# Second MLP product of a token mixer in eight pairs of token blocks instead of two whole blocks and seven pairs

## The chip, the cores and the metric

The kernel runs on one core of one Trainium2 chip. The metric is the device time of one execution in microseconds; the profile is that of one such execution, and its times count from the first instruction of the span.

## What is computed

The reference modulates and normalizes a sequence x of S = 2048 tokens by D = 640 channels, adds a gated state-space block (A), normalizes again and adds a gated MLP over the token axis (B). The change is in block B:

```python
h = _layernorm(x, axis=-1)                                  # (B, S, D)
u = jnp.einsum("bsd,sf->bdf", h, w1) + b1                  # (B, D, F)
u = _gelu(u)
y = jnp.einsum("bdf,fs->bds", u, w2) + b2                  # (B, D, S)
...
x = x + gb * _B_ref(h, B_w1, B_b1, B_w2, B_b2)
```

with F = 1728. All data is float32.

## The kernel before

A float32 product is made of three matmuls on rounded operands: each operand is split into a rounded part (`hi`, written as F32R by ScalarE) and a rest (`lo`, the difference, by VectorE), and hi x hi, hi x lo and lo x hi are added up in PSUM. Every matmul here has a stationary block of 128x128 and 320 moving columns, that is half of the 640 channels.

**First product.** U, F by D, is made in 14 blocks of F. The normalized tokens stand in SBUF as 16 pairs of tiles `H[j]` (hi and lo) of 640 columns each; H[0] to H[2], H[9] to H[11] lie in a tile named `r_z`, H[3] to H[5] in `r_v`, H[6] to H[8] in `h_a`, H[12] to H[15] in `h_x`. The loop over `FS` makes blocks 4 to 12, one after another (96 matmuls each: 16 j, 3 steps, 2 halves; in the loop's round for block 6 the blocks 6 and 13 are made together). The weights of the next block are loaded into the tile `X` and split meanwhile (`load_w`, `split_w`). `u_evac` takes a block's sums from PSUM through the GELU and stores U[f] as hi and lo, for each half of the channels.

**Second product.** The output is made of 16 token blocks s of 128 tokens. Before the change the first NW = 2 of them are whole blocks: 14 blocks of F, 3 steps, 2 halves, 84 matmuls each (line 1121). The other 14 are made in NP = 7 pairs. A pair, times two halves of F (blocks 0 to 6 and 7 to 13) and two halves of the channels, is a 2 by 2 block product, and is done with seven half-size products instead of eight. Their stationary sides are A11, A12, A22 (blocks of w2) and sums of blocks S1 to S4 (`sums`); their moving sides are parts of U and, for S1, S2, S3 and A22, sums of parts of U, the sets `TU[i]`, i = 0 to 6. One such product is 7 sets by 3 steps, 21 matmuls (line 1057), so a pair has 147.

A set i is made from U[i] and U[7 + i] by `t_sums`: two sums of the upper part, one of the lower, three differences. It has four tiles of 320 columns, held as two pairs: the first serves S1 and S3, the second S2 and A22. There is no room for the sets while H is in use. So sets 6, 0, 1, 2, 3 (`SAVED`) are made during blocks 7 to 11 and written to a DRAM tensor `ts` (`t_save`), whole. Sets 0 to 3 are loaded back into tiles of H (`t_back`) when the last block (f = 12) has read these, and split there during the last block and the first whole token block (`t_split`); sets 4 and 5 are made and split at once (`t_make`). Set 6 is loaded behind the whole blocks (lines 1127 to 1129).

The order on each engine is the order of the code; nothing reorders it. SyncE issues the loads and stores one after another, and each waits, in this queue, for the tile that it writes to be free. For product n, `prep` splits the stationary side into one of three slots (ScalarE, then VectorE), two products ahead. `outcome` takes the product from PSUM, and `finish` (VectorE) adds the bias, multiplies by the gate, adds x (loaded back by `x_load` from DRAM tensor `xs`) and stores a quarter of a pair. PSUM has four slots of two banks, used in turn.

Of the kernel before, what the change touches and what calls it, by code (L numbers as in the profile page):

```python
# [50 lines left out]
def mixer_kernel(ctx: ExitStack, tc: tile.TileContext, q, k, v, shift_k, ssm_k, ssm_D, w1, b1, w2, b2, c,  # L51
# [16 lines left out]
    ts = drp.tile([5 * 128, 1280], F32, name="ts")  # L68
# [315 lines left out]
    NF, NW = 14, 2  # L384
    FS = (4, 5, 6, 7, 8, 9, 10, 11, 12)
    WB = {i: n % 2 for n, i in enumerate(FS + tuple(range(NF, NF + NW)))}
# [3 lines left out]
    f14 = lambda t: t[:, 0:1792].rearrange("p (f m) -> p f m", f=14)  # L390

    def load_w2(t, s, f0, n):

        for h in range(n // 7 or 1):
            o = 7 * h
            sync.dma_start(t[:, o:o + 6, :], dram(w2, fo(f0 + o) * S + 128 * s, [[S, 128], [128 * S, 6], [1, 128]]))
            sync.dma_start(t[:, o + 6, :], dram(w2, fo(f0 + o + 6) * S + 128 * s, [[S, 128], [1, 128]]))

    def load_w(i, t=X):
        if i is None:  # L400
            return
        if i < NF:
            t = j16(t)
            for b in range(2):
                sync.dma_start(t[64 * b:64 * b + 64],
                               dram(w1, 16 * b * F + fo(i), [[32 * F, 64], [F, 16], [1, 128]]))
            raw[i] = (t, [slice(0, 8), slice(8, 16)])
        else:
            t = f14(t)
            load_w2(t, i - NF, 0, 14)  # L410
            raw[i] = (t, [slice(0, 7), slice(7, 14)])
# [14 lines left out]
    def split_w(i, t2=None, eng=dve):  # L426
        if i is None:
            return
        if t2 is None:
            t2 = T_wb[WB[i]]  # L430
        view = j16 if i < NF else f14
        hi, lo = view(t2[:, 0:2048]), view(t2[:, 2048:4096])
# [247 lines left out]
    acc = []  # L680
# [160 lines left out]
    right = thirds(mem("xb", 5120, "u_x"), 14)  # L841
# [33 lines left out]

    def t_sums(i):

        t, w_, u, (hi, lo) = m_p[:, 0:640], m_p[:, 768:2048], U[i], full[7 + i]
        TT(dve, w_[:, 0:320], u[0], u[2], ALU.add)
        TT(dve, w_[:, 320:640], u[1], u[3], ALU.add)  # L880
        TT(dve, w_[:, 640:1280], hi, lo, ALU.add)
        TT(dve, two_(t), span2(w_, 320, 640), span2(w_, 0, 320), ALU.subtract)
        TT(dve, w_[:, 960:1280], w_[:, 960:1280], t[:, 0:320], ALU.subtract)
        TT(dve, w_[:, 640:960], w_[:, 640:960], w_[:, 960:1280], ALU.subtract)
        return two_(t), two_(w_[:, 640:1280])
# [7 lines left out]
    def t_back(i):  # L893

        n = SAVED.index(i)
        for k in range(2):
            sync.dma_start(span2(H[JS[i][k]][0], 320, 640), ts[128 * n:128 * n + 128, 640 * k:640 * k + 640]
                           .rearrange("p (h m) -> p h m", h=2))

    def t_split(i, whole=None):  # L900

        for k in range(2):
            hi, lo = (span2(H[JS[i][k]][0], o, 640) for o in (0, 320))
            act.activation(hi.bitcast(F32R), whole[k] if whole else lo, AF.Copy)
        for k in range(2):
            hi, lo = (span2(H[JS[i][k]][0], o, 640) for o in (0, 320))
            TT(dve, lo.bitcast(F32R), whole[k] if whole else lo, hi, ALU.subtract)

    def t_make(i):
        t_split(i, t_sums(i))  # L910
# [8 lines left out]
    after = dict(zip(FS, FS[1:] + tuple(range(NF, NF + NW))))  # L919
    after.update({i: i + 1 for i in range(NF, NF + NW - 1)})  # L920
# [45 lines left out]
    NP = (16 - NW) // 2  # L966
# [3 lines left out]
    def load_pair(p, n0=0, n1=4):  # L970

        if p < NP:
            for n in range(n0, n1):
                w_ = ("A11", "A21", "A22", "A12")[n]
                A[p, w_] = place[(4 * p + n) % 8]
                load_w2(A[p, w_], NW + 2 * p + int(w_[1] == "2"), 7 * int(w_[2] == "2"), 7)

    for f_ in FS:
# [5 lines left out]
        load_w(13 if f_ == 4 else nxt(n_))  # L984
        if f_ == 6:
            m_p = ends(sets)
            continue
# [6 lines left out]
        if f_ == FS[-1]:  # L994
            m_v = mem("v", 4520, "m_v")
            place = [q7(t, o + 896 * i) for t, n, o in ((m_v, 5, 0), (X, 2, 0), (m_p, 1, 1152)) for i in range(n)]
# [10 lines left out]
    m_w, slots = [], []  # L1007
    S1 = q7(m_p, 0)
    W, bank = {}, {}
    Q = lambda n, i: U[7 * (n // 2) + i]  # L1010
    moving = {"A11": lambda i: Q(0, i)[0::2], "A12": lambda i: Q(2, i)[0::2], "S4": lambda i: Q(2, i)[1::2],
              "S1": lambda i: TU[i][0], "S2": lambda i: TU[i][1], "S3": lambda i: TU[i][2], "A22": lambda i: TU[i][3]}
    ORDER = ("A11", "A12", "S1", "S2", "S3", "S4", "A22")

    def x_load(s, h, t):
        sync.dma_start(t, xs[128 * s:128 * s + 128, 320 * h:320 * h + 320])

    def x_pair(p):
        if p < NP:
            for n in range(4):  # L1020
                x_load(NW + 2 * p + n // 2, n % 2, xq[4 * (p % 2) + n])

    def sums(n):

        p, w_ = n // 7, ORDER[n % 7]
        if p >= NP:
            return
        a = lambda k: A[p, k]
        if w_ == "S1":
            A[p, w_] = S1  # L1030
            TT(dve, S1, a("A21"), a("A22"), ALU.add)
        elif w_ == "S2":
            TT(dve, a("A21"), a("A11"), a("A21"), ALU.subtract)
            TT(dve, a("A11"), S1, a("A11"), ALU.subtract)
            A[p, "S3"], A[p, "S2"] = a("A21"), a("A11")
        elif w_ == "S4":
            TT(dve, a("A12"), a("A12"), a("S2"), ALU.subtract)
            A[p, "S4"] = a("A12")

    def prep(n):  # L1040

        p, w_ = n // 7, ORDER[n % 7]
        if p < NP:
            W[n] = slots[n % 3]
            act.activation(W[n][0].bitcast(F32R), A[p, w_], AF.Copy)  # L1045
            TT(dve, W[n][1].bitcast(F32R), A[p, w_], W[n][0], ALU.subtract)

    def product(n):
        w_ = ORDER[n % 7]
        if n > 4 or n % 2 == 0:  # L1050
            bank["t"] = psum()
        bank[n] = bank["t"][:, 0:320] if n > 3 or n % 2 == 0 else bank["t"][:, 512:832]
        wh, wl = W.pop(n)
        for i in range(7):
            rh, rl = moving[w_](i)
            for k, (w, r) in enumerate(((wh, rh), (wh, rl), (wl, rh))):
                pe.matmul(bank[n], w[:, i].bitcast(F32R), r.bitcast(F32R), start=i == 0 and k == 0,  # L1057
                          stop=i == 6 and k == 2)
# [12 lines left out]
    def outcome(n):  # L1071

        p, w_ = n // 7, ORDER[n % 7]
        t, s, x = bank.pop(n), NW + 2 * p, xq[4 * (p % 2):4 * (p % 2) + 4]
# [8 lines left out]
        elif w_ == "S3":  # L1083
            TT(dve, u3, t, u2, ALU.add)
            TT(dve, u2, u2, p5, ALU.add)
            finish(s + 1, 1, u3, o4, x[3], p5)
# [3 lines left out]
        elif w_ == "S4":  # L1090
            finish(s, 1, t, o2, x[1], u2)
        elif p == NP - 1:
            finish(s + 1, 0, t, o3, u3)
        else:
            finish(s + 1, 0, t, o3, x[2], u3)

    acc = []
    for s in range(NW):
        i = NF + s
        acc.append(psum().rearrange("p (h m) -> p h m", h=2))  # L1100
        split_w(nxt(i))
        load_w(nxt(nxt(i)))
        if s == 0:
            t_make(5)
            t_split(1)
        if s == NW - 1:
            load_pair(1, 0, 3)
            m_w.append(mem(f"w{WB[NF + NW - 2]}", 4096, "m_w0"))
            slots += [(q7(m_w[0], 1792 * i), q7(m_w[0], 1792 * i + 896)) for i in range(2)]
            t_split(2)  # L1110
            t_split(3)
            prep(0)
            prep(1)
            sums(2)
            sums(3)
        wh, wl = blk[i]
        for f_ in range(NF):
            u = U[f_]
            for k, (w, r) in enumerate(((wh, 0), (wh, 2), (wl, 0))):
                for h in range(2):  # L1120
                    pe.matmul(acc[s][:, h, 0:320], w[:, f_].bitcast(F32R), u[r + h].bitcast(F32R),  # L1121
                              start=f_ == 0 and k == 0, stop=f_ == NF - 1 and k == 2)
    m_w.append(mem(f"w{WB[NF + NW - 1]}", 4096, "m_w1"))
    t_ = thirds(m_w[1], 7, 1792) + thirds(m_w[0], 1, 3584)
# [70 lines left out]
```

## Time and profile before

| | us |
|---|---|
| three runs before, median | 698.0 |
| lowest, highest | 696.08, 701.78 |
| profiled execution, its own time | 701.14 |
| its span, first to last instruction | 699.4 |
| last block of the first product (f = 12) ends | 518.0 |
| two whole token blocks (L1121) | 518.0 to 542.7 |
| seven pairs (L1057) | 542.7 to 695.4 |

The mean granted clock of TensorE was 0.974. A row of the timeline has the start, the length, the engine, the line of the code, the operation, the tiles written and read, the shapes and the count, and in brackets how long the engine sat idle before it and what ended that. PE is TensorE, PEld its weight loads, DVE VectorE, ACT ScalarE, POOL GpSimd, SPq the DMA issues of SyncE; L60 is the line of a helper that records every two-operand sum. A row of the windows has the busy time of PE, PEld, DVE, ACT and POOL, each with its count, then the granted clock of TensorE, the share of the DMA engines' time that was busy, and the GB/s that they moved.

### The profile page before, as it was taken

The numbers are of one execution on the slowest core, as the hardware profiler recorded it, in microseconds if no ns is written. First come the engines' busy times: TensorE is split into PE (matmuls) and PEld (weight loads), VectorE is DVE, ScalarE is ACT, GpSimd is POOL, SyncE is SP. The second block draws the span as 40 slices with busy tenths as digits, with TensorE's granted clock in tenths as the row PEclk, the third lists the DMA queues.
The fourth block names the chain that finished last, engine by engine and source line by source line (L and its number), as shares of the span: only waits on it lengthen the run. The fifth ranks groups of instructions, "written<-read, shape, count | busy, mean of one in ns | idle before, by whom it ended". The sixth has DMA issues, their size and how long they took to land.

```text
span 699.4 us, 20705 instructions
## 1 busy us (share of the span) xinstructions
PE 642.1 (92%) x9078; PEld 621.7 (89%) x9078; DVE 499.2 (71%) x844; ACT 308.1 (44%) x463; POOL 155.3 (22%) x137
## 2 busy tenths in 40 slices
PE   0699978899999999987899999999999999999997
PEld 0699678889999999777899999999999999999997
DVE  6778569849779837888895420563477698888886
ACT  0664574435645645555776421521333333333331
POOL 5297049614715626300000000000000000000000
PEclk9999899889999999989899999999999999999999
DMA  9978988527242523352022641466284734455511
GB/s 180 206 217 242 340 164 167 118 47 156 52 79 69 186 60 93 116 121 62 21 40 54 129 92 30 98 133 161 91 254 134 221 115 129 141 172 172 160 49 39
DMA packets 170848, 89.36 MB, mean 128 GB/s; under 512 B 89571, under 2 KB 160518, under 8 KB 170758
## 3 DMA queue, kind: packets, MB, share of 16 engines
q1 hardware_dynamic: 166210, 86.73, 49.2%
q10 hardware_dynamic: 4548, 1.31, 1.1%
q8 instruction: 71, 1.16, 0.7%
q14 instruction: 19, 0.16, 0.1%
HBM read 74.25 MB, written 13.76 MB: 126 GB/s over the span
## 4 chain that ended last, share of the span: by engine, by line
PE 66%; DVE 14%; POOL 8%; ACT 4%; issue 3%; SPq 2%; DMA 2%; ACTq 0%; DVEq 0%; POOLq 0%
PE pst L1057 21%; PE pst L446 17%; PE pst L230 7%; POOL y L60 6%; PE pst L275 5%; PE pst L246 5%; PE pst L1121 4%; PE pst L945 3%; DVE tap L60 3%; PE pst L294 2%; DVE kt L60 2%; POOL t L60 1%; SPq L164 1%; DMA in<-in_A_k_dram 1%; PE tap L354 1%
## 5 line engine op out<-in xcount | busy, mean ns | idle before, releaser
L246 PEld LDWEIGHTS pst<-z,w 128*64 128x64 f32 x2560 | 94.8, 141 | 8.6 <-ACT z L232 7.3
L246 PE MATMUL pst<-z,w 128*64 128x64 f32 x2560 | 95.8, 240 | 7.1 <-ACT z L232 6.1
L60 POOL TENSOR_TENSOR y<-p 128x256 f32<-128x256 f32 x72 | 91.7, 1327 | 23.2 <-DVE p L60 22.9
L60 DVE TENSOR_TENSOR p<-pst,kt 128x512 f32<-128x512 f32 x80 | 52.8, 691 | 23.6 <-ACT kt L250 14.3
L230 PE MATMUL pst<-v,x 128*64 128x128 f32 x640 | 46.7, 308 | 23.6 <-DVE x L60 23.6
L230 PEld LDWEIGHTS pst<-v,x 128*64 128x64 f32 x640 | 44.7, 221 | 24.1 <-POOL t L471 23.6
L232 ACT ACTIVATE z<-pst 128x1024 f32<-128x1024 f32 x40 | 46.0, 1149 | 40.2 <-PE pst L230 21.8
L1057 PE MATMUL pst<-r_z,m_w 128*128 128x320 f32 x259 | 48.5, 309 | 1.5 <-DVE m_w L60 1.5
L275 PEld LDWEIGHTS pst<-v,y 32*128 32x128 f32 x1280 | 41.9, 203 | 7.3 <-POOL y L60 4.4
L275 PE MATMUL pst<-v,y 32*128 32x64 f32 x1280 | 43.9, 290 | 4.1 <-DVE y L60 3.2
L1045 ACT ACTIVATE m_w<-m_v 128x896 fp32r<-128x896 f32 x30 | 27.8, 948 | 43.1 <-DVE m_v L60 27.6
L250 ACT ACTIVATE kt<-pst 128x512 f32<-128x512 f32 x40 | 25.0, 625 | 46.5 <-PE pst L246 24.2
L1057 PEld LDWEIGHTS pst<-r_z,m_w 128*128 128x128 f32 x259 | 40.6, 188 | 1.7 <-DVE m_w L60 1.7
L60 DVE TENSOR_TENSOR m_w<-m_v,m_w 128x896 fp32r<-128x896 f32 x30 | 32.5, 1087 | 11.2 <-ACT m_w L1045 10.8
L230 PE MATMUL pst<-v,p 128*64 128x128 f32 x640 | 37.3, 274 | 2.2 <-ACT p L176 1.6
L230 PEld LDWEIGHTS pst<-v,p 128*64 128x64 f32 x640 | 35.0, 137 | 3.2 <-ACT p L176 1.7
L851 ACT ACTIVATE pst<-pst,sm 128x640 f32<-128x640 f32 x14 | 10.7, 767 | 59.0 <-PE pst L446 59.0
L60 DVE TENSOR_TENSOR tap<-tap,kt 128x512 f32<-128x512 f32 x51 | 35.6, 698 | 1.3
L60 DVE TENSOR_TENSOR kt<-in,tap 128x512 f32<-128x512 f32 x51 | 35.0, 687 | 1.5
L1057 PE MATMUL pst<-h_x,m_w 128*128 128x320 f32 x168 | 33.7, 309 | 0.0
L283 ACT ACTIVATE z<-pst 128x512 f32<-128x512 f32 x38 | 21.4, 664 | 27.1 <-PE pst L275 27.1
L1045 ACT ACTIVATE m_w<-m_p 128x896 fp32r<-128x896 f32 x13 | 12.4, 954 | 44.2 <-DVE m_p L60 27.7
(309 smaller groups left out, 1401.2 us busy)
## 6 DMA issues: line engine op xcount, KB each, us to landing
x<-in_B_w_dram SPq DMA_DIRECT2D x20, 512.0 KB
m_v<-in_B_w_dram SPq DMA_DIRECT2D x19, 384.0 KB
aux<-in_A_ssm_k_dram SPq DMA_DIRECT2D x10, 512.0 KB
m_x<-xs SPq DMA_DIRECT2D x32, 160.0 KB
out_dram<-m_x SPq DMA_DIRECT2D x32, 160.0 KB
in<-in_A_k_dram SPq DMA_DIRECT2D x36, 128.0 KB
in<-in_A_v_dram SPq DMA_DIRECT2D x36, 128.0 KB
x<-in_B_w_dram SPq DMA_DIRECT2D x10, 384.0 KB
```

The lines of the kernel that those rows point to most:

```text
L60: TT = lambda eng, o, a, b, op: eng.tensor_tensor(o, a, b, op=op)
L230: pe.matmul(ps[64 * ri:64 * ri + 64, o:o + 128], lhs, F1[:, 128 * ri:128 * ri + 128], start=True, stop=True)
L232: evac = lambda: act.activation(Z[:, side, t].rearrange("p a k e -> p e a k"), ps.rearrange("p (e a k) -> p e a k", a=8, e=2), AF.Copy)
L246: pe.matmul(ps[64 * h:64 * h + 64, o:o + 64], W2[k1 // 32][:, 2 * (k1 % 32) + ri], rhs, start=True, stop=True)
L250: act.activation(kt.rearrange("p (m i) -> p m i", i=32), pv[:, :, 1], AF.Copy)
L275: pe.matmul(pp[qd // 2][:, o:o + 64], Y[p, ri, i:i + 2].rearrange("p i k -> p (i k)"), V2[p, 64 * ri:64 * ri + 64], start=ri == 0, stop=ri ...
L283: act.activation(o, i, AF.Copy)
L446: pe.matmul(ps[0:m, h, 0:320], w_.bitcast(F32R), r_[:, 320 * h:320 * h + 320].bitcast(F32R), start=first and i == 0, stop=last and i == 2)
L945: pe.matmul(ps[n][:, h, 0:320], sets[n][:, j].bitcast(F32R), r[:, 320 * h:320 * h + 320].bitcast(F32R), start=j == 0 and r is hh, stop=j = ...
L1045: act.activation(W[n][0].bitcast(F32R), A[p, w_], AF.Copy)
L1057: pe.matmul(bank[n], w[:, i].bitcast(F32R), r.bitcast(F32R), start=i == 0 and k == 0, stop=i == 6 and k == 2)
L1121: pe.matmul(acc[s][:, h, 0:320], w[:, f_].bitcast(F32R), u[r + h].bitcast(F32R), start=f_ == 0 and k == 0, stop=f_ == NF - 1 and k == 2)
```

## The change

There are no whole token blocks any more: all 16 token blocks are made in eight pairs (`NP = 8`). The seven products of a pair take the sets in the order 6, 0, 1, 2, 3, 4, 5.

The five saved sets are now split before they are saved: `t_save` rounds both pairs of tiles on ScalarE into spare columns, subtracts on VectorE, and writes rounded part and rest to `ts`, which has twice the columns. `t_back` loads half a set, 1280 columns in one piece, and nothing is split after it. Of the two sets made around the last block, set 4 is made in its round of the loop and set 5 behind it. A11 and A12 of pair 0 are loaded already in the round of block 11, into `X`. Set 6 goes into the tile `m_x`, which takes the place of the upper half of U once `t_upper(5)` has read it. All of this, and the first three `prep`, stands in the code of the last block's round. The output tiles o2, o3 and o4 are gone; `p5`, `u2`, `u3` are stored from instead. Each product has a PSUM slot of its own from the start.

```diff
-    ts = drp.tile([5 * 128, 1280], F32, name="ts")
+    ts = drp.tile([5 * 128, 2560], F32, name="ts")
...
     def t_save(i):
         n = SAVED.index(i)
-        for k, t in enumerate(t_sums(i)):
-            sync.dma_start(ts[128 * n:128 * n + 128, 640 * k:640 * k + 640].rearrange("p (h m) -> p h m", h=2), t)
+        t_upper(i)
+        t_sums(i)
+        for t, hi in zip((T13, T42), his):
+            act.activation(hi.bitcast(F32R), t, AF.Copy)
+        for k, (t, hi) in enumerate(zip((T13, T42), his)):
+            TT(dve, t.bitcast(F32R), t, hi, ALU.subtract)
+            for o, p in ((0, hi), (320, t)):
+                sync.dma_start(dram(ts, 2560 * 128 * n + 1280 * k + o, [[2560, 128], [640, 2], [1, 320]]), p)
+
+    def t_back(i, k):
+        t, n = H[JS[i][k]][0], SAVED.index(i)
+        sync.dma_start(bass.AP(tensor=t.tensor, offset=t.offset, ap=[t.ap[0], [1, 1280]]),
+                       ts[128 * n:128 * n + 128, 1280 * k:1280 * k + 1280])
...
-    NP = (16 - NW) // 2
+    NP = 8
...
+        if f_ == 11:
+            load_pair(0, 0, 2)
...
         if f_ == FS[-1]:
-            t_back(0)
-            t_back(1)
-            load_pair(0)
-            t_back(2)
-            t_back(3)
-            t_make(4)
-            t_split(0)
+            t_back(0, 0)
+            load_pair(0, 2, 4)
+            for i in range(7):
+                t_back(*((0, 1), (1, 0), (1, 1), (2, 0), (2, 1), (3, 0), (3, 1))[i])
+            prep(0)
+            t_upper(4)
+            t_sums(4)
+            t_split(4)
+            prep(1)
+            t_upper(5)
+            m_x = mem("xb", 5120, "m_x")
+            slots.append((q7(m_x, 0), q7(m_x, 896)))
+            t_, n = thirds(m_x, 8, 1792), SAVED.index(6)
+            TU[6] = [(t_[2 * i], t_[2 * i + 1]) for i in (0, 3, 1, 2)]
+            sync.dma_start(m_x[:, 1792:4352], ts[128 * n:128 * n + 128])
+            sums(2)
+            prep(2)
+            sums(3)
         u_evac(f_, ps)
+    t_sums(5)
+    t_split(5)
...
+    x_pair(0)
+    load_pair(1, 0, 2)
+    x_pair(1)
...
-        for i in range(7):
+        for m, i in enumerate(SETS):
...
-            finish(s + 1, 1, u3, o4, x[3], p5)
+            finish(s + 1, 1, u3, p5, x[3], p5)
...
-            finish(s, 1, t, o2, x[1], u2)
+            finish(s, 1, t, u2, x[1], u2)
...
-    for s in range(NW):
...
-        for f_ in range(NF):
-            u = U[f_]
-            for k, (w, r) in enumerate(((wh, 0), (wh, 2), (wl, 0))):
-                for h in range(2):
-                    pe.matmul(acc[s][:, h, 0:320], w[:, f_].bitcast(F32R), u[r + h].bitcast(F32R),
...
     for n in range(7 * NP):
...
-        if n not in (0, 2):
-            for i in range(n - (n in (1, 3)), n + 1):
-                outcome(i)
-        if n == 1:
-            for k in range(4):
-                finish(NW - 2 + k // 2, k % 2, acc[NW - 2 + k // 2][:, k % 2, 0:320], (o2, o4, o3, o1)[k], xq[4 + k])
+        outcome(n)
```

SyncE's queue from the first load of a saved set on, before. `r_z`, `h_a` and `h_x` are tiles of H, `m_v` takes the place of `r_v` and holds blocks of w2:

```order
L897 DMA r_z<-ts 128x2x320
L897 DMA h_a<-ts 128x2x320 x3
L396 DMA m_v<-in_B_w2_dram 128x6x128
L397 DMA m_v<-in_B_w2_dram 128x128
L396 DMA m_v<-in_B_w2_dram 128x6x128
L397 DMA m_v<-in_B_w2_dram 128x128
L396 DMA m_v<-in_B_w2_dram 128x6x128
L397 DMA m_v<-in_B_w2_dram 128x128
L396 DMA m_v<-in_B_w2_dram 128x6x128
L397 DMA m_v<-in_B_w2_dram 128x128
L897 DMA r_z<-ts 128x2x320 x3
L897 DMA h_x<-ts 128x2x320
```

The same place of the changed kernel, up to the x rows of pair 0. `m_x` is set 6, `m_w_6261` the x rows:

```order
L897 DMA r_z<-ts 128x1280
L393 DMA m_v<-in_B_w2_dram 128x6x128
L394 DMA m_v<-in_B_w2_dram 128x128
L393 DMA m_v<-in_B_w2_dram 128x6x128
L394 DMA m_v<-in_B_w2_dram 128x128
L897 DMA h_a<-ts 128x1280 x3
L897 DMA r_z<-ts 128x1280 x3
L897 DMA h_x<-ts 128x1280
L1050 DMA m_x<-ts 128x2560
L981 DMA m_w_6261<-xs 128x320 x4
```

The two later blocks of w2 (A21 and A22) stand behind one half set, and behind them seven half sets and then set 6.

TensorE at the start of the third product of the first pair, S1, before. `pst_6523` is its place in PSUM; `m_w_6435` holds its stationary side and, in the last row, set 6 too:

```order
L1057 MATMUL pst_6523<-r_z,m_w_6435 128x320 x3
L1057 MATMUL pst_6523<-h_a,m_w_6435 128x320 x3
L1057 MATMUL pst_6523<-r_z,m_w_6435 128x320 x9
L1057 MATMUL pst_6523<-h_x,m_w_6435 128x320 x3
L1057 MATMUL pst_6523<-m_w_6435 128x320 x3
```

The end of product A12 and the product S1 of the changed kernel:

```order
L1071 MATMUL pst_6299<-u_y,m_w_6214 128x320 x6
L1071 MATMUL pst_6299<-h_x,m_w_6214 128x320 x3
L1071 MATMUL pst_6328<-m_x 128x320 x3
L1071 MATMUL pst_6328<-r_z,m_x 128x320 x3
L1071 MATMUL pst_6328<-h_a,m_x 128x320 x3
L1071 MATMUL pst_6328<-r_z,m_x 128x320 x9
L1071 MATMUL pst_6328<-h_x,m_x 128x320 x3
```

Set 6 was the last set of S1 and is now the first; set 5 (in `h_x`) is the last.

More of the change, by code (lines that the diff above doesn't have):

```diff
@@ L401, in load_w @@
             return
[L402 to L411, printed above, removed]
+        t = j16(t)
+        for b in range(2):
+            sync.dma_start(t[64 * b:64 * b + 64],
+                           dram(w1, 16 * b * F + fo(i), [[32 * F, 64], [F, 16], [1, 128]]))
+        raw[i] = (t, [slice(0, 8), slice(8, 16)])
     def load_rows(r, t):
@@ L874, in span2, with t_upper @@
         return bass.AP(tensor=t.tensor, offset=t.offset + o, ap=[t.ap[0], [step, 2], [1, 320]])
+    def t_upper(i):
+        u = U[i]
+        TT(dve, TW[:, 0:320], u[0], u[2], ALU.add)
+        TT(dve, TW[:, 320:640], u[1], u[3], ALU.add)
     def t_sums(i):
[L878 to L881, printed above, removed]
@@ L918, in mixer_kernel @@
     raw6_ = raw.pop(6)[0]
-    after = dict(zip(FS, FS[1:] + tuple(range(NF, NF + NW))))
-    after.update({i: i + 1 for i in range(NF, NF + NW - 1)})
+    after = dict(zip(FS, FS[1:]))
     nxt = lambda i: after.get(i)
@@ L973, in load_pair, with x_load, x_pair, sums @@
             for n in range(n0, n1):
-                w_ = ("A11", "A21", "A22", "A12")[n]
+                w_ = ("A11", "A12", "A21", "A22")[n]
                 A[p, w_] = place[(4 * p + n) % 8]
-                load_w2(A[p, w_], NW + 2 * p + int(w_[1] == "2"), 7 * int(w_[2] == "2"), 7)
+                load_w2(A[p, w_], 2 * p + int(w_[1] == "2"), 7 * int(w_[2] == "2"))
+    W, bank, slots, place = {}, {}, [], [q7(X, 0), q7(X, 896)]
+    Q = lambda n, i: U[7 * (n // 2) + i]
+    moving = {"A11": lambda i: Q(0, i)[0::2], "A12": lambda i: Q(2, i)[0::2], "S4": lambda i: Q(2, i)[1::2],
+              "S1": lambda i: TU[i][0], "S2": lambda i: TU[i][1], "S3": lambda i: TU[i][2], "A22": lambda i: TU[i][3]}
+    SETS = (6, 0, 1, 2, 3, 4, 5)
+    ORDER = ("A11", "A12", "S1", "S2", "S3", "S4", "A22")
+    of = lambda n: (n // 7, ORDER[n % 7])
+    def x_load(s, h, t):
+        sync.dma_start(t, xs[128 * s:128 * s + 128, 320 * h:320 * h + 320])
+    def x_pair(p):
+        if p < NP:
+            for n in range(4):
+                x_load(2 * p + n // 2, n % 2, xq[4 * (p % 2) + n])
+    def sums(n):
+        p, w_ = of(n)
+        if p >= NP:
+            return
+        a = lambda k: A[p, k]
+        if w_ == "S1":
+            A[p, w_] = S1 if p else place[6]
+            TT(dve, A[p, w_], a("A21"), a("A22"), ALU.add)
+        elif w_ == "S2":
+            TT(dve, a("A21"), a("A11"), a("A21"), ALU.subtract)
+            TT(dve, a("A11"), a("S1"), a("A11"), ALU.subtract)
+            A[p, "S3"], A[p, "S2"] = a("A21"), a("A11")
+        elif w_ == "S4":
+            TT(dve, a("A12"), a("A12"), a("S2"), ALU.subtract)
+            A[p, "S4"] = a("A12")
+    def prep(n):
+        p, w_ = of(n)
+        if p < NP:
+            W[n] = slots[n % 3]
+            act.activation(W[n][0].bitcast(F32R), A[p, w_], AF.Copy)
+            TT(dve, W[n][1].bitcast(F32R), A[p, w_], W[n][0], ALU.subtract)
     for f_ in FS:
@@ L1013, in mixer_kernel @@
[L1013 to L1046, printed above, removed]
+            m_v, m_w0 = mem("v", 4520, "m_v"), mem(f"w{WB[11]}", 4096, "m_w0")
+            place += [q7(m_v, 896 * i) for i in range(5)] + [q7(m_p, 1152)]
+            slots += [(q7(m_w0, 1792 * i), q7(m_w0, 1792 * i + 896)) for i in range(2)]
```

119 lines of the change are left out of this document (30 added, 89 removed).

## The prediction

> **What bounds the kernel now.** I read the page's busy times first, then the chain of waits from 500 us on, then the windows of that stretch, and last the timelines of the engines and of the DMA queue around the last block of the first product. Page, busy time of TensorE:
>
> ```profile
> PE 642.1 (92%) x9078; PEld 621.7 (89%) x9078; DVE 499.2 (71%) x844; ACT 308.1 (44%) x463; POOL 155.3 (22%) x137
> ```
>
> 92% is an average, so the stage has to be looked at by itself. The chain of waits from 500 us (start, length, what):
>
> ```profile
> 499.98 18.04 PE pst L446 x123
> 518.02 24.65 PE pst L1121 x168
> 542.68 6.17 PE pst L1057 x42
> 548.85 0.02 issue
> 548.87 1.09 DVE m_w L60
> ...
> 551.51 3.08 DMA out_dram<-m_x
> ...
> 555.60 1.09 DVE m_w L60
> 556.70 0.04 issue
> 556.74 138.70 PE pst L1057 x943
> 695.44 0.02 issue
> 695.47 0.56 DVE m_x L1064
> ```
>
> The two whole token blocks (L1121) and the seven pairs (L1057) are TensorE end to end: 943 matmuls in 138.70 us are **0.147 us** each, and 168 in 24.65 us are the same. The chain leaves TensorE once, at 548.87. Windows (busy us by engine, then granted clock, DMA share, GB/s):
>
> ```profile
> 434.00:488.00 54.00, 54.00 (x370) 54.00 (x370) 29.53 (x42) 18.03 (x24) 0.00 (x0) 1.00 0.54 122
> 503.90:518.00 14.10, 14.10 (x98) 14.10 (x97) 9.48 (x13) 6.11 (x8) 0.00 (x0) 1.00 0.65 200
> 518.00:530.00 12.00, 12.00 (x84) 12.00 (x83) 10.22 (x15) 7.87 (x12) 0.00 (x0) 1.00 1.01 281
> 548.80:556.80 8.00, 6.55 (x46) 6.29 (x44) 7.56 (x14) 1.32 (x3) 0.00 (x0) 1.00 0.67 223
> ```
>
> TensorE is full up to 548.8; from 548.8 to 556.8 it lacks 1.45 us. The timeline of TensorE names the wait:
>
> ```profile
> 556.74 0.41 PE L1057 MATMUL pst<-r_z,m_w 128*128 128x320 f32 x1 [1.45 <-DVE m_w L60]
> ```
>
> So the kernel is bound by the number of matmuls here, and the transition, which is what the change rewrites, costs 1.45 us today. The window from 518 to 530 matters most: the DMA engines are full (share 1.01) while two whole blocks hide it.
>
> **Removed work.** The eighth pair has 7 products of 21 matmuls, 147, where two whole blocks have 168: 21 x 0.147 = **-3.1 us**. The order of the changed kernel has 1,176 such matmuls after the last block instead of 1,197, so this part does happen. The four `finish` calls of the whole blocks go from VectorE, and with them the chain 548.87 to 556.74: **-1.45 us**. If nothing new waits, that is -4.5.
>
> **Added while the first product runs.** Five times, a save takes two copies on ScalarE and two subtractions on VectorE more, of 128x640, and its DMA doubles to 1.31 MB. Prices (timelines of ScalarE and VectorE):
>
> ```profile
> 503.98 0.77 ACT L851 ACTIVATE pst<-pst,sm 128x640 f32<-128x640 f32 x1 [10.68 <-PE pst L446]
> 505.52 0.82 DVE L60 TENSOR_TENSOR u_y<-pst,u_y 128x640 fp32r<-128x640 f32 x1 [7.32 <-ACT u_y L856]
> 514.59 0.74 ACT L904 ACTIVATE r_z<-r_z 128x640 fp32r<-128x640 f32 x1 [1.85 <-PE pst L446]
> ```
>
> That is 1.5 us of ScalarE and 1.6 of VectorE for each block of 14.1 us of TensorE. VectorE is 55% and ScalarE 33% busy from 434 to 488, and the DMA engines 54%. The split of the next block's weights stands ahead of the save on both engines, so nothing that TensorE wants is behind it. I cost it at nothing; if that cover were gone it would be up to 1.6 us a block.
>
> **The transition.** It moves under the last block (f = 12), which starts at 503.9, since ScalarE gets the block before it at 503.98, and ends at 518.0. Then come products A11 and A12, 42 matmuls, to 524.2. Product S1 is next, and its first matmul takes set 6, the last one in the queue of SyncE. So the question is when set 6 lands. Sets go into the tiles of H, which the last block frees one after another, 6 matmuls for each j. W2 blocks A21 and A22 go into the tile of H[3] to H[5], free after 36 matmuls, 503.9 + 5.3 = 509.2. Queue and wait prices, and rates (timelines, then windows):
>
> ```profile
> 542.71 0.37 SPq L1127 DMA_DIRECT2D m_w<-ts  x1
> 545.80 0.74 ACT L1138 ACTIVATE m_w<-m_w 128x640 fp32r<-128x640 f32 x1 [2.09 <-DMA m_w<-ts]
> 68.00:78.00 10.00, 9.36 (x166) 7.11 (x166) 9.66 (x30) 6.26 (x10) 0.00 (x0) 0.75 1.03 398
> 82.00:86.00 4.00, 4.00 (x134) 3.71 (x133) 0.00 (x0) 1.38 (x4) 0.00 (x0) 1.00 0.98 394
> 84.00:86.00 2.00, 2.00 (x65) 1.71 (x61) 0.00 (x0) 0.39 (x1) 0.00 (x0) 1.00 1.03 424
> ```
>
> A lone load of 0.33 MB took 3.1 us from issue to use; less 0.8 for the bytes, 2.3 are fixed. A21 and A22 are 0.92 MB in 512-byte rows: at the 281 GB/s of the window 518 to 530, 3.3 us, so they land at 509.2 + 2.3 + 3.3 = 514.7. Behind them stand seven half sets of 0.66 MB and set 6 of 1.31 MB, 5.9 MB, all issued by about 516 (the last tile, H[12], is free at 515.4). The rate is not known for this shape: each row is now 5 KB or more, where the sets of before came in pieces of 1.3 KB. The near rows are 398 GB/s (loads of q, 2.5 KB rows) and 394 (a constant table); the far one is the 281 of sets and weights mixed, at this very place. I take 394, because long rows made those two: 15.0 us, **landing at 529.7**, TensorE waiting **5.5 us**. At 281 it is 21.0 us, 535.7, and a wait of 11.5. I see no way below 4 us: even the 424 GB/s of the best 2 us of that table makes 13.9.
>
> What else S1 wants is earlier. On VectorE and ScalarE the prices are (timelines):
>
> ```profile
> 496.32 1.88 DVE L60 TENSOR_TENSOR m_p<-m_p 128x640 f32<-128x640 f32 x3
> 511.82 1.77 DVE L60 TENSOR_TENSOR r_z<-m_p,r_z 128x640 fp32r<-128x640 f32 x2
> 518.06 0.77 ACT L851 ACTIVATE pst<-pst,sm 128x640 f32<-128x640 f32 x1 [1.84 <-PE pst L446]
> 518.86 0.70 ACT L856 ACTIVATE h_x<-pst 128x640 fp32r<-128x640 f32 x1
> 530.44 1.78 ACT L1045 ACTIVATE m_w<-m_v 128x896 fp32r<-128x896 f32 x2
> 531.95 2.09 DVE L60 TENSOR_TENSOR m_w<-m_v,m_w 128x896 fp32r<-128x896 f32 x2
> 533.95 1.08 DVE L60 TENSOR_TENSOR m_p<-m_v 128x896 f32<-128x896 f32 x1
> ```
>
> VectorE from 506.3: rest of A11 1.1, upper sums of set 4 0.8, lower 2.7 (0.82 + 1.88), copy and split 1.7, rest of A12 1.1, upper sums of set 5 0.8: 514.5. There it meets A22 at 514.7: sum S1 1.1, ScalarE's copy 0.9, rest 1.1, two sums 2.2: 520.0. The rest of U[12] makes 520.8, and A12 wants it only at its 20th matmul, 521.1 + 2.8 = 523.9. Set 5 follows: sums 2.7, copy 0.7, split 1.7: 525.9, against S1's last three matmuls, after 532. This cover has 3 us at U[12] and 6 at set 5. ScalarE's copy of S1 stands ahead of the GELU of the last block, so a late A22 would delay both; at 281 GB/s it is in time.
>
> **After the wait** the x rows of pair 0 (0.66 MB, behind set 6) hold VectorE in A12's `finish` to about 532; behind that add stand the rest of S3 and the sum and rest of S4, ready by 537, while TensorE, with S1 from 529.7 and the clock below, gets to S3 at about 537.6 and to S4 at 540.7. So no second wait. The four output tiles become one and three reused ones; each is written again at least five products (15 us) after its store, and the store above took 3.08 us: nothing. The tail after the last matmul is unchanged.
>
> **The clock.** A wait of 5.5 us is longer than the 1.45 of today. Timeline and windows of an earlier wait:
>
> ```profile
> 349.86 0.90 PE L446 MATMUL pst<-h_a,wb 128*128 128x320 f32 x2 [2.77 <-ACT h_a L743]
> 347.00:349.40 2.40, 0.09 (x1) 0.00 (x0) 1.59 (x9) 0.63 (x2) 0.22 (x1) 1.00 0.45 114
> 349.40:352.80 3.40, 2.94 (x11) 2.94 (x12) 3.33 (x8) 3.40 (x7) 0.00 (x0) 0.50 1.19 216
> 352.80:356.00 3.20, 3.20 (x24) 3.20 (x23) 2.53 (x8) 1.00 (x4) 0.80 (x2) 1.00 0.08 13
> ```
>
> After 2.77 us without a matmul the granted clock was 0.50 for 3.4 us, and then 1.00; after the 1.45 us it stayed at 1.00. So the wait should cost half of 3.4, **+1.7 us**, more; bounds 0 and 3.4 (two such stretches). The Trainium skill ("TensorE: Matmul & The Clock Gate", section "What's actually happening") says that the clock halves after at least one idle window of about 3.4 us and comes back after one busy window. By that rule a wait under 3.4 us would be free, while the trace shows that 2.77 us already was enough, so here the rows decide; at 5.5 us both give the same.
>
> **The sum** against the profiled run (701.14 us, of which 699.4 is the span): -3.1 - 1.45 + 5.5 + 1.7 = +2.7, so 703.8. That run is 3.1 over the median of the three (698.0), which I take as run-to-run spread; the forecast on the median is **700.7 us**. The Trainium skill ("HBM Reference", its table of bandwidths and the paragraph under it) gives a core's share as about 358 GB/s and about 425 for a core that streams alone; by 358 an estimate from that page is 1.5 us more. The two windows above, at 394 and 398, lie above that share and below the other figure, so the trace does not bear the lower one out.
>
> **Rivals.** 1% of the median is 7 us, about what a measurement can tell, so the bounds are 691 and 705.
> - *Nothing waits.* If the queue delivered set 6 ahead of the half sets, or they came much sooner, the gain stays: 693.4. For it: A11 and A12 give 6.2 us of cover. Against: 5.9 MB between 514.7 and 524.2 would be 620 GB/s. Chance 0.12. It is also the floor: TensorE has no more to give.
> - *The sets come at the pace that this place shows now.* At 281 GB/s the wait is 11.5 and the clock takes 1.7 to 3.4: +8.7 to +10.4, so 706.7 to 708.4, slower by over 1%. For it: the sets of before were part of that window, from the same DRAM tensor, at a DMA share of 1.01. Against: half of its bytes were 512-byte rows of W2. It decides from about 306 GB/s down (5.9 MB in 19.3 us, a wait of 9.8). Chance 0.25, of which 0.20 past the bound.
> - *VectorE and ScalarE are late instead*, through A22: set 5 would take over from set 6 only if A22 came after about 521, six us late. Up to +3 more, 703.7. Chance 0.08.
>
> **How the numbers follow.** The forecast has 0.55, with 698 to 703 as its own range (424 GB/s and no clock loss; 370 GB/s and two stretches of half clock). Faster by over 1% lies below the floor, so only a spread of runs could show it: 0.03. Slower: 0.20. Within 1%: 0.77. The range goes from the floor, 694, to the middle of the second rival, 707.5.
>
> **What would show it.** Right: TensorE idle once, between A12 and S1, released by a DMA from `ts`, 4 to 7 us, with a row of 0.50 behind it; no idle after S2; 1,176 matmuls. Wrong: an idle time released by VectorE or ScalarE, a wait under 3 us or over 9, the clock at 1.00 right through, or matmuls in the steady part further apart than 0.147 us.

## The result, and the profile after

| | before | after |
|---|---|---|
| median of four executions each, us | 698.1 | 709.3 |
| lowest, highest | 696.1, 701.8 | 707.8, 713.2 |
| ratio, 95% interval | | 1.0136 (1.0087 to 1.0184) |
| profiled execution, its own time | 701.14 | 707.75 |
| its span | 699.4 | 706.0 |

The changed kernel is slower. Two runs of it below, of 22 executions, show less of a loss than these four, 1.0059 and 1.0078. The busy time of TensorE fell and its share fell more, on the page of the changed kernel:

```profile
PE 636.4 (90%) x9057; PEld 616.2 (87%) x9057; DVE 511.0 (72%) x857; ACT 312.4 (44%) x467; POOL 155.5 (22%) x137
```

21 matmuls fewer, as the change says. The chain of waits of the changed kernel, where the two whole blocks and the finish stall stood:

```profile
383.51 28.43 PE pst L437 x192
...
512.66 4.38 DMA m_v<-in_B_w_dram
517.82 15.05 DMA m_x<-ts
...
533.01 169.04 PE pst L1071 x1134
```

A DMA of 15.05 us, set 6 from `ts`, is now a link of the chain, with the load of A22 ahead of it (in the first repeat below it is the issue of the last half set). What is behind it is TensorE end to end: 1,134 matmuls and, with A11 and A12, the 1,176 of the order. The timeline of TensorE around it (start, length, what, and in brackets the idle time ahead):

```profile
516.71 3.24 PE L437 MATMUL pst<-h_x,wb0b 128*128 128x320 f32 x21
519.79 0.31 PE L1071 MATMUL pst<-u_i,m_w 128*128 128x320 f32 x1
...
533.01 1.14 PE L1071 MATMUL pst<-m_x 128*128 128x320 f32 x3 [6.90 <-DMA m_x<-ts]
533.95 1.00 PE L1071 MATMUL pst<-r_z,m_x 128*128 128x320 f32 x3
534.75 1.00 PE L1071 MATMUL pst<-h_a,m_x 128*128 128x320 f32 x3
```

The last block ends at 519.79, A11 and A12 follow without a gap, and S1 waits **6.90 us** for set 6. Its first matmuls then run at little more than half speed: three in 0.80 us (from 533.95 to 534.75), 0.27 each, where three take 0.44 at 0.147. The windows of the changed kernel show the clock:

```profile
519.80:526.10 6.30, 6.30 (x44) 6.05 (x42) 6.13 (x9) 2.32 (x4) 0.00 (x0) 1.00 1.02 421
526.10:533.00 6.90, 0.01 (x1) 0.02 (x1) 3.46 (x5) 2.63 (x4) 0.00 (x0) 0.65 1.03 397
533.00:538.50 5.50, 5.49 (x21) 5.50 (x22) 2.50 (x3) 0.00 (x0) 0.00 (x0) 0.50 1.05 295
538.50:702.05 163.55, 163.53 (x1115) 163.27 (x1114) 137.41 (x195) 53.53 (x66) 0.00 (x0) 1.00 0.42 127
```

S1's 21 matmuls take 5.49 us at a granted clock of 0.50, where 21 x 0.147 is 3.1: the half clock costs **2.4 us**. Behind it TensorE is full to the end: there is no second wait.

Where the 6.6 us between the two spans come from is seen by cutting both at a mark that the change doesn't touch, the start of the first product's dense part (381.58 in the chain of before, 383.51 in that of after). Windows of before and then of after:

```profile
381.58:699.40 317.82, 312.39 (x2125) 311.76 (x2125) 206.76 (x294) 102.83 (x137) 0.00 (x0) 1.00 0.48 130
```

```profile
383.51:706.00 322.49, 311.63 (x2104) 311.13 (x2104) 218.43 (x307) 107.21 (x141) 0.00 (x0) 0.98 0.52 148
```

Behind the mark the change costs 322.49 - 317.82 = **+4.7 us**, and the terms give -3.1 - 1.45 + 6.9 + 2.4 = +4.75. The other 1.9 us lie ahead of the mark, in code that is the same. So from here on I compare two numbers of each run: the time from the mark to the end, and the timed ratio.

### The profile page after: what moved, and what is told of

The parts are those of the page before. It is cut to its first block, busy times and chain, and to the rows that moved or that the text cites. A ratio compares the mean times of both kernels' runs of the same rounds, so it can differ in the third digit from the quotient of the medians.

```text
span 706.0 us, 20714 instructions
## 1 busy us (share of the span) xinstructions
PE 636.4 (90%) x9057; PEld 616.2 (87%) x9057; DVE 511.0 (72%) x857; ACT 312.4 (44%) x467; POOL 155.5 (22%) x137
## 4 chain that ended last, share of the span: by engine, by line
PE 56%; DVE 15%; DMA 7%; POOL 7%; SPq 7%; ACT 4%; issue 3%; ACTq 0%; DVEq 0%; POOLq 0%
PE pst L1071 24%; PE pst L437 16%; POOL y L60 6%; PE pst L275 5%; PE pst L939 3%; PE pst L230 3%; DVE tap L60 3%; SPq L506 3%; DVE kt L60 3%; PE pst L246 3%; PE pst L294 2%; DMA m_x<-ts 2%; DMA in<-in_A_k_dram 2%; DMA aux<-in_w_mod_dram 2%; SPq L164 2%
## 5 line engine op out<-in xcount | busy, mean ns | idle before, releaser
L60 DVE TENSOR_TENSOR p<-pst,kt 128x512 f32<-128x512 f32 x80 | 53.0, 694 | 22.5 <-ACT kt L250 13.1
L1071 PE MATMUL pst<-r_z,m_w 128*128 128x320 f32 x198 | 37.1, 309 | 0.0
L1071 PEld LDWEIGHTS pst<-r_z,m_w 128*128 128x128 f32 x198 | 31.1, 188 | 0.0
L1010 ACT ACTIVATE m_w<-m_v 128x896 fp32r<-128x896 f32 x19 | 17.9, 948 | 24.1 <-DVE m_v L60 12.1
L294 PEld LDWEIGHTS pst<-z,v 64*64 64x64 f32 x1280 | 22.0, 142 | 6.7 <-issue 3.3
L437 PE MATMUL pst<-r_z,wb 128*128 128x320 f32 x144 | 22.7, 312 | 4.5 <-ACT r_z L734 2.8
L294 PE MATMUL pst<-z,v 64*64 64x64 f32 x1280 | 23.9, 228 | 3.0 <-issue 1.7
L1071 PE MATMUL pst<-h_x,m_w 128*128 128x320 f32 x132 | 26.5, 309 | 0.0
```

The lines of the kernel that those rows point to most:

```text
L60: TT = lambda eng, o, a, b, op: eng.tensor_tensor(o, a, b, op=op)
L294: pe.matmul(ps[64 * b:64 * b + 64, 512 * e + 64 * jj:512 * e + 64 * jj + 64], V1[p, ri, n2], T2[p, :, 32 * ri + n2], start=ri == 0, stop=r ...
L437: pe.matmul(ps[0:m, h, 0:320], w_.bitcast(F32R), r_[:, 320 * h:320 * h + 320].bitcast(F32R), start=first and i == 0, stop=last and i == 2)
```

## The experiments

**The changed kernel again.** Two runs without an edit, of 10 and 12 executions.

> The changed kernel once more, unedited, beside before on one chip. Theory A (the loss is made in the transition: TensorE waits 6.9 us for set 6 and then runs 5.5 us at half clock): 3 to 10 us over before, the profiled wait again 6 to 8 us, half clock for 1 to 3 stretches of 3.4 us. Rival B (half of the measured loss is spread of the first 383 us, whose code is the same in both): the medians come closer to the profiled pair, +4 to +6 us, and the first 383 us differ by 2 us or more between profiles.

> The changed kernel unaltered, timed once more. If its loss is the 3.8 to 4.7 us that the two profiles show between the start of the first product's dense part and the end, it is 1.004 to 1.008 of before, as in e0_again, and the 1.0136 of the first measurement was a draw of four executions from a wide spread. If the first 383 us, whose code is the same, are slower in it by themselves, it is 1.010 or more again, and its span up to that point is longer than before's 381.6 by 2 us or more.

Measured: 1.0059 (1.0015 to 1.0103) and 1.0078 (1.0036 to 1.0121). The stretches behind the mark and TensorE's wait, from the windows and the timeline of the first, then of the second:

```profile
383.19:704.80 321.61, 311.55 (x2104) 311.05 (x2104) 218.40 (x307) 107.24 (x141) 0.00 (x0) 0.99 0.53 149
531.92 1.14 PE L1071 MATMUL pst<-m_x 128*128 128x320 f32 x3 [6.12 <-DMA m_x<-ts]
531.90:537.20 5.30, 5.28 (x20) 5.30 (x21) 2.49 (x3) 0.00 (x0) 0.00 (x0) 0.50 1.14 320
```

```profile
384.87:707.60 322.73, 311.22 (x2104) 310.72 (x2104) 218.43 (x307) 107.23 (x141) 0.00 (x0) 0.99 0.52 148
535.01 1.14 PE L1071 MATMUL pst<-m_x 128*128 128x320 f32 x3 [7.54 <-DMA m_x<-ts]
535.00:539.50 4.50, 4.49 (x17) 4.50 (x18) 2.50 (x3) 0.00 (x0) 0.00 (x0) 0.50 0.98 277
```

The same story with other sizes. At 0.147 each, the 20 and 17 matmuls in the windows at 0.50 would take 2.9 and 2.5 us instead of 5.28 and 4.49, so the clock costs 2.3 and 2.0. The terms make -4.55 + 6.12 + 2.3 = +3.9 and -4.55 + 7.54 + 2.0 = +5.0; the stretches are +3.8 and +4.9 against 317.8. The wait varies by 1.4 us between three executions of one kernel, and the work done at half clock by 1.0 us. Of the first expectation both parts came out: behind the mark the transition makes the loss (Theory A), and the medians came closer to the profiled pair, with a first part that varies by itself (Rival B). The second expectation had two marks for a first part that is slower by itself, and they disagree: its profile has the mark at 384.87, 3.3 us behind that of before, but the ratio stayed under 1.010. The marks of all ten profiles lie between 377.7 and 386.7, three of the edited kernels' ahead of before's 381.58 by 1 us or more, so no lean of the changed code shows in them.

**No loads of sets.**

```diff
-            t_back(0, 0)
...
-            for i in range(7):
-                t_back(*((0, 1), (1, 0), (1, 1), (2, 0), (2, 1), (3, 0), (3, 1))[i])
...
-            TU[6] = [(t_[2 * i], t_[2 * i + 1]) for i in (0, 3, 1, 2)]
-            sync.dma_start(m_x[:, 1792:4352], ts[128 * n:128 * n + 128])
+            TU[6] = TU[0]
```

> Leaves out all loads of saved sets; set 6 is read from set 0's place, so the sums are wrong data. Theory A: no wait between A12 and S1, clock 1.00 there, and the gain of 3.1 + 1.45 us stands: 693 to 694 where before has 698. Rival C (the doubled saves during the first product, or the rest of the moved work, cost as much as the wait): 698 or more although nothing waits for the loads.

Measured: 0.9954 (0.9910 to 0.9997). Window behind the mark and chain:

```profile
386.68:699.40 312.72, 308.93 (x2104) 308.66 (x2104) 218.11 (x307) 107.25 (x141) 0.00 (x0) 1.00 0.49 132
523.13 172.49 PE pst L1066 x1176
```

Without the loads all 1,176 matmuls follow on each other, in 172.49 us, 0.147 each, and the stretch is 5.1 us shorter than before's, near the 4.5 that the prediction gives as the floor. The timed ratio is worth 3.2 us, and its interval runs from 0.2 to 6.3. Everything else of the change is still in this kernel: the five longer saves, the sums and splits under the last block, the x rows, the four output tiles. None of it costs TensorE anything that shows.

**Unused matmuls during the wait.**

```diff
+        if n == 2:
+            spin = psum()
+            for _ in range(40):
+                pe.matmul(spin[:, 0:320], U[0][0][:, 0:128].bitcast(F32R), U[0][2].bitcast(F32R), start=True, stop=True)
```

> As the changed kernel, with 40 matmuls whose result is not used (5.9 us) between A12 and S1. Theory A: TensorE idles only about 1 us there, the clock stays at 1.00, S1 starts when it did (set 6 lands at the same time) and runs in 3.1 us instead of 5.5: about 2.4 us faster than the run of the unedited kernel beside it. Rival D (the half clock costs nothing, or comes from elsewhere): the same time as the unedited kernel.

> The kernel of e2_warm once more, timed beside e4 on one chip: 40 unused products of U[0] stand between A12 and S1, so that the granted clock can't fall while set 6 is awaited. If the half clock is worth the 1.9 to 2.8 us by which its stretch was shorter than those of after (319.7 against 321.6 and 322.5), it is 1.002 to 1.005 of before and 0.995 to 0.998 of the changed kernel; if the clock costs nothing, it is 1.006 as the changed kernel was. e4 ahead of it by 3 to 6 us in the stretch, if the waits are what is left.

Measured: 1.0052 (1.0010 to 1.0094) and 1.0032 (0.9994 to 1.0069). Windows behind the mark of the first, its unused matmuls and S1 in the timeline, and the window of S1:

```profile
382.12:701.80 319.68, 315.01 (x2144) 314.52 (x2144) 218.39 (x307) 107.23 (x141) 0.00 (x0) 1.00 0.53 150
524.56 6.03 PE L1118 MATMUL pst<-u_t 128*128 128x320 f32 x40
531.32 0.67 PE L1071 MATMUL pst<-m_x 128*128 128x320 f32 x3 [0.74 <-DMA m_x<-ts]
531.30:534.40 3.10, 3.08 (x21) 3.10 (x22) 2.49 (x3) 0.00 (x0) 0.00 (x0) 1.00 1.20 305
```

and, of the second, the window behind the mark and the start of S1:

```profile
379.71:698.80 319.09, 315.02 (x2144) 314.52 (x2144) 218.34 (x307) 107.26 (x141) 0.00 (x0) 1.00 0.53 150
528.33 0.68 PE L1071 MATMUL pst<-m_x 128*128 128x320 f32 x3 [0.16 <-DMA m_x<-ts]
```

With TensorE kept busy the clock stays at 1.00 and S1 takes 3.1 us again. The stretches, 319.7 and 319.1, are 2.9 us under the mean of the three of the changed kernel (322.3). From the end of A12 to S1 these two profiles have 6.6 and 6.0 us, the unused matmuls and the short wait behind them; that is 0.5 us less on average than the three waits of the changed kernel. The other 2.4 us are the half clock, whose price by the rows was 2.0 to 2.4. Timing doesn't show it: the first of the two kernels was 0.4 us faster than the unedited one beside it (703.8 and 704.2), where 2.4 were expected, and though the second came out at 1.0032, within the 1.002 to 1.005 expected, the intervals of the ratios overlap with those of the changed kernel. So the price rests on the profiles.

**Set 6 summed last.**

```diff
-    SETS = (6, 0, 1, 2, 3, 4, 5)
+    SETS = (0, 1, 2, 3, 4, 5, 6)
```

> Order of sets 0, 1, 2, 3, 4, 5, 6 instead of 6 first; the loads stand in the same order. Theory A: S1 starts with the sets that have landed, waits about 1 us for set 3 and about 3 us for set 6 at its end, only its last three matmuls are behind it: the end comes 2.6 us earlier by the order and up to 2.4 us more by the clock, so 3 to 5 us faster than the unedited kernel. Rival E (another wait is right behind, on x of pair 0 or on VectorE): less than 2 us, with an idle time at S3.

Measured: 1.0033 (0.9987 to 1.0079). Window behind the mark, and the two waits of S1 in the timeline:

```profile
377.73:697.20 319.47, 311.92 (x2104) 311.13 (x2104) 218.39 (x307) 107.35 (x141) 0.00 (x0) 0.99 0.53 150
522.15 1.15 PE L1071 MATMUL pst<-r_z,m_x 128*128 128x320 f32 x6 [0.51 <-DMA r_z<-ts]
526.84 1.17 PE L1071 MATMUL pst<-m_x 128*128 128x320 f32 x3 [3.10 <-DMA m_x<-ts]
526.80:532.30 5.50, 5.46 (x20) 5.46 (x21) 3.59 (x4) 1.39 (x2) 0.00 (x0) 0.50 1.07 305
```

S1 does 18 of its 21 matmuls ahead of set 6, 18 x 0.147 = 2.6 us, and little more than that is won: the waits together are 3.6 us, and the half clock still takes 2.5 (20 matmuls in 5.46 us instead of 2.9), since 3.10 us without work were enough for it here. The stretch is 2.1 us shorter than that of the unedited kernel beside it, where 3 to 5 were expected; the part by the clock did not come. Nothing waits at S3, the sign of Rival E. Set 6 in the last place of the queue is late even for the last place in S1.

**The loads in the order of use.**

```diff
-    SETS = (6, 0, 1, 2, 3, 4, 5)
+    SETS = (0, 1, 2, 3, 4, 5, 6)
...
-            for i in range(7):
-                t_back(*((0, 1), (1, 0), (1, 1), (2, 0), (2, 1), (3, 0), (3, 1))[i])
+            for i in (1, 2, 3):
+                t_back(i, 0)
...
-            sync.dma_start(m_x[:, 1792:4352], ts[128 * n:128 * n + 128])
+            m_w1 = mem(f"w{WB[12]}", 4096, "m_w1")
+            p1, p5, u2, u3, o1, *xq = thirds(m_w1, 10, 896) + thirds(m_p, 3)
+            sync.dma_start(m_x[:, 1792:3072], ts[128 * n:128 * n + 128, 0:1280])
+            x_load(0, 0, xq[0])
+            for i in range(4):
+                t_back(i, 1)
+            sync.dma_start(m_x[:, 3072:4352], ts[128 * n:128 * n + 128, 1280:2560])
...
-    m_w1 = mem(f"w{WB[12]}", 4096, "m_w1")
-    p1, p5, u2, u3, o1, *xq = thirds(m_w1, 10, 896) + thirds(m_p, 3)
...
-    x_pair(0)
+    for n in (1, 2, 3):
+        x_load(n // 2, n % 2, xq[n])
```

> The same bytes are loaded, but in the order in which the products use them: the sums of the sets are taken 0 to 6, the five saved sets come with their first halves (those that A11 to S1 read) ahead of the second ones, set 6 is cut in two in the same way, and x[0] of pair 0 stands between. Theory A (the wait for set 6 by the DMA queue, and the half clock behind it, make up the loss): S1's three sums of a set each come later than their halves land, so the wait ahead of S1 falls from 6.1 and 6.9 us to at most 2 us in pieces, the granted clock stays at 1.00, and the stretch from the start of the first product's dense part to the end takes 313.5 to 316 us (after 322.5 and 321.6 in its two profiles, before 317.8); timed, 0.993 to 1.000 of before. Rival (the bytes themselves cost, by contention with TensorE's reads or with the x rows): the stretch stays at 319 us or more, and the time at 1.003 or more of before, though the wait ahead of S1 goes.

Measured, beside the second run with unused matmuls: 695.7 us against 700.7 of before, 0.9932 (0.9891 to 0.9973). Windows and timeline:

```profile
378.76:693.90 315.14, 309.80 (x2104) 308.68 (x2104) 218.22 (x307) 107.33 (x141) 0.00 (x0) 1.00 0.54 152
515.10:526.10 11.00, 10.52 (x71) 10.18 (x70) 10.35 (x15) 5.40 (x8) 0.00 (x0) 1.00 1.02 415
525.89 0.71 PE L1076 MATMUL pst<-r_z,m_w 128*128 128x320 f32 x3 [0.48 <-DMA r_z<-ts]
527.47 0.70 PE L1076 MATMUL pst<-h_x,m_w 128*128 128x320 f32 x3 [0.87 <-DMA h_x<-ts]
```

The same bytes, with the DMA engines as full (share 1.02) and TensorE working beside them: the wait of 6.1 to 7.5 us gives way to two short ones in S2, 1.35 us together, the clock stays at 1.00, and the loss turns into a gain. So the bytes cost little by themselves: the stretch is 2.4 us longer than without any loads, 1.35 of it in these waits. This kernel is faster than before, and by the ratios, which were taken on different chips, than the changed kernel.

**Set 6 ahead of the second halves only.**

```diff
-            for i in range(7):
-                t_back(*((0, 1), (1, 0), (1, 1), (2, 0), (2, 1), (3, 0), (3, 1))[i])
+            for i in (1, 2, 3):
+                t_back(i, 0)
...
             sync.dma_start(m_x[:, 1792:4352], ts[128 * n:128 * n + 128])
+            for i in range(4):
+                t_back(i, 1)
```

> The smallest mend of the changed kernel: set 6 is still summed first and loaded whole, but its load is issued ahead of the second halves of sets 0 to 3 (2.6 MB, of which S1 reads nothing) instead of behind them. Theory A, at the 372 GB/s of the profiled execution: set 6 lands about 7 us earlier, 6 to 8 us behind the end of block 12, where A11 and A12 end after some 6.3 us; so the wait ahead of S1 falls to at most 2 us, the second halves land while S1 is computed and cost S2 at most 2 us, and the clock stays at 1.00. From the start of the first product's dense part to the end: 314 to 317 us; timed, 0.993 to 1.000 of before and within 0.4% of e4_in_use_order. If e4 gained by its other edits (the order of the sums, set 6 in two parts, x[0] ahead), this stays at 319 us or more and 1.002 or more.

Measured, beside the second run of the unaltered changed kernel: 698.5 us against 700.1, 0.9986 (0.9943 to 1.0028), and the changed kernel 706.1 on the same chip. Window and timeline:

```profile
380.61:695.20 314.59, 309.55 (x2104) 308.69 (x2104) 217.97 (x307) 107.12 (x141) 0.00 (x0) 1.00 0.54 152
529.00 0.71 PE L1073 MATMUL pst<-h_x,m_w 128*128 128x320 f32 x3 [0.90 <-DMA h_x<-ts]
```

S1 starts without a wait; S2 waits 0.90 us for the last second half, and S3 0.17 us for VectorE. Behind the mark this is 0.5 us shorter than the kernel with four edits, so the place of set 6's load in the queue is what decides, and the order of the sums, the cut of set 6 and the earlier x row add nothing that shows. On the same chip it is 7.7 us faster than the changed kernel. The timed ratios of the two mended kernels are 0.5% apart, more than I expected, and their intervals overlap; by them, a gain over before is shown for the kernel with four edits alone.

## Why the prediction was wrong

The path, the wait and what ends it were right. Two terms of the sum were too small, and the range left out how far single measurements of these kernels spread.

- *The removed work*, -3.1 and -1.45: right. The stretch without loads came out 5.1 us shorter than before's, where 4.55 were named.
- *The saves, at nothing*: right (no loads, same saves, no idle time).
- *The term of 5.5 us for set 6 was mis-sized*: 6.90, 6.12 and 7.54 us in three profiles. In the first, set 6 landed 13.1 us behind the end of the last block (517.82 + 15.05 = 532.87 against 519.79), where 11.7 were predicted (529.7 and 518.0). 0.5 us of the 1.4 were a later A22: it landed at 512.66 + 4.38 = 517.04, 2.75 ahead of the block's end, against 3.3. The rest is the rate. The 5.9 MB took 532.87 - 517.04 = 15.83 us, 373 GB/s to the landing instead of 394. Over this stretch the windows of the changed kernel say more:

```profile
517.10:520.00 2.90, 2.90 (x22) 2.90 (x21) 1.86 (x2) 0.96 (x2) 0.00 (x0) 1.00 0.97 363
520.00:525.00 5.00, 5.00 (x36) 5.00 (x35) 4.86 (x7) 1.52 (x3) 0.00 (x0) 1.00 1.02 422
525.00:530.00 5.00, 1.11 (x8) 0.85 (x6) 4.52 (x7) 3.42 (x5) 0.00 (x0) 0.82 1.03 430
530.00:532.90 2.90, 0.00 (x0) 0.00 (x0) 0.01 (x1) 0.00 (x0) 0.00 (x0) 0.50 1.02 352
```

These add up to 2.9 x 363 + 5 x 422 + 5 x 430 + 2.9 x 352 = 6.33 MB. The engines moved 401 GB/s, better than the 394 that I took from the rows of before, but not all of it was the sets. The packets in the trace can be told apart by their length: 10,240 bytes for set 6, 5,120 for the half sets, 1,280 for x rows, 512 for weights. By them 0.8 MB were x rows and weights that stand behind set 6 in the queue, and 0.3 MB of the half sets had already gone before A22 landed. The first x row went at 529.54, 2.8 us before the last packet of set 6 ended at 532.36, so some engines were done with their part of set 6, and on with what stands behind it, while others were still at it. The variation of the wait lies there too: 90% of set 6's packets had ended 10.8 to 10.9 us behind the end of the last block in all three profiles, the last one 12.6, 11.8 and 13.2 us behind it, for waits of 6.90, 6.12 and 7.54. The Trainium skill ("DMA: Bandwidth & Descriptors", section "Why a DMA increments its semaphore by 16 and not by 1") says that a transfer runs on up to 16 engines that finish independently, and that it has landed when the last has. The packet times agree with that, though the trace doesn't name the engine of a packet.
- *The term of 1.7 us for the half clock was mis-sized*: 2.4, 2.3 and 2.0. I took one stretch of 3.4 us at half clock behind the wait, as it stood in the trace of before; 4.5 to 5.5 us of work ran at 0.50. Within the range that I gave for it (0 to 3.4). Two windows of the changed kernel hold the changes of the clock:

```profile
528.00:530.00 2.00, 0.00 (x0) 0.00 (x0) 1.97 (x3) 0.73 (x1) 0.00 (x0) 0.56 1.00 418
538.00:540.00 2.00, 2.00 (x14) 2.00 (x14) 0.00 (x0) 1.17 (x2) 0.00 (x0) 0.88 0.89 252
```

A mean of 0.56 puts the fall at 528.2, and 0.88 the return at 538.5: 10.2 us, three stretches of 3.4. In the first TensorE was idle, in the second S1 began (533.0), the third was busy throughout. In the traces of the two repeats the clock was at 0.50 from 530.4 to 537.2 and from 532.7 to 539.6, two stretches each, and S1 began in the first of them. So the work at half clock was the rest of the stretch in which S1 began and one whole stretch more, in all three.
- *No second wait*: right. Counted from the end of the last block, the x rows held VectorE for 13.6 us, where about 14 were said, and TensorE did not wait for that. Timeline of VectorE in the changed kernel, U[12], the end of set 5, and the x row:

```profile
522.37 0.82 DVE L60 TENSOR_TENSOR h_x<-pst,h_x 128x640 fp32r<-128x640 f32 x1
...
525.88 1.71 DVE L60 TENSOR_TENSOR h_x<-m_p,h_x 128x640 fp32r<-128x640 f32 x2
...
533.43 0.49 DVE L60 TENSOR_TENSOR m_w<-m_w 128x320 f32<-128x320 f32 x1 [3.42 <-DMA m_w<-xs]
```

- *The rivals.* Nothing waits: no, and the run without loads shows what it would have been. 281 GB/s: no, with 373; the first result passed 705 without it. VectorE and ScalarE late: no.

By its own steps the sum should have been +3.9 to +5.0 instead of +2.7, 702 to 703 on a median of 698, which is within the range. The two mis-sized terms are thus worth 1.2 to 2.3 of the 8.6 us between the forecast of 700.7 and the first result of 709.3. The other 6 us don't come back in the 22 later executions, whose ratios are worth 4 and 5.5 us. The range was made of the terms alone; single executions of before go from 695.4 to over 706 in the runs here, and of the unaltered changed kernel from 697.9 to over 710. That spread is the likely source, but four executions at 707.75 or more are still an unlikely draw from it: five of the 22 later ones reach that. The two profiled executions of the changed kernel that do, the first and that of the second repeat, have 1.9 and 3.3 us of their excess over before ahead of the mark. For the other three of the first four there is no profile, so where their 6 us lie stays open. The part ahead of the mark varies much by itself. The longest and the shortest of ten profiles, windows of the run without loads and of the one with set 6 last, whose code up to there differs in nothing:

```profile
24.00:386.68 362.68, 333.50 (x6951) 314.38 (x6948) 273.77 (x517) 202.90 (x326) 142.58 (x121) 0.94 0.49 119
```

```profile
24.00:377.73 353.73, 322.37 (x6953) 302.93 (x6949) 273.37 (x518) 202.77 (x326) 141.22 (x121) 0.98 0.49 122
```

9 us, more than all that the change does, at granted clocks of 0.94 and 0.98. The longer one is the one at the lower clock, but the clock doesn't explain all of it. The same windows of the changed kernel and of the one with the loads in the order of use:

```profile
24.00:383.51 359.51, 324.23 (x6952) 304.48 (x6948) 273.95 (x517) 202.12 (x326) 142.39 (x121) 0.97 0.49 120
```

```profile
24.00:378.76 354.76, 328.11 (x6953) 308.74 (x6954) 274.16 (x518) 203.42 (x326) 141.73 (x121) 0.96 0.50 123
```

Here the longer one, by 4.75 us, has the higher clock. What else lengthens this part stays open.

## What to carry to other kernels

Work that hides a transfer is worth more than its own time: the two whole blocks looked like 3.1 us of extra matmuls, and were the cover for the loads of the sets, 5.9 MB of them in the changed kernel. When such cover goes, put the loads into the queue in the order in which they are read, and look first at the load that is read first: moving one load of set 6 ahead of four half sets took the 6.1 to 7.5 us of wait down to 0.9. And cut a trace at a mark that the change doesn't touch before a difference of spans is explained.

## What was not expected of the hardware

The same short wait can be followed by the half clock or not. In before, 2.77 us without a matmul were followed by 3.4 us at 0.50 (the row in the prediction); in the changed kernel the same wait, at the same place, was not. Timeline and window:

```profile
351.79 2.47 PE L437 MATMUL pst<-h_a,wb 128*128 128x320 f32 x15 [2.75 <-ACT h_a L734]
351.80:355.20 3.40, 3.40 (x23) 3.40 (x24) 3.33 (x8) 3.40 (x6) 0.00 (x0) 1.00 1.01 184
```

2.75 us, and 1.00 behind it. The Trainium skill ("TensorE: Matmul & The Clock Gate", section "What's actually happening") says that the gate watches a free-running window, and that the point at which the clock changes depends on where in the window the work begins. The two rows agree with that: 2.77 and 2.75 us, with different outcomes. With set 6 last, 3.10 us were enough for the half clock once more. The Trainium skill's window of about 3.4 us (same section) as the least idle time is not borne out: 2.77 and 3.10 are under it. And what follows a long wait is not one stretch at half clock but 4.5 to 5.5 us of work, in all three profiles.
